# A state update on four groups of array columns, its sum in four pieces, and a new order of the steps

## The chip, the cores and the metric

The kernel runs on one core of a Trainium2 chip. A core has TensorE (matrix products into PSUM; PE in a profile, its weight loads PEld), VectorE (DVE), ScalarE (ACT), GpSimd (POOL) and SyncE (SP), which issues nearly all transfers here. The metric is the device time in microseconds of one launch, lower is better.

## The reference, cut to what matters

Inputs are `q, k, v, a_re, a_im` of shape (4, 8, 768, 48): batch, heads, time, width. A gated linear attention runs over time, and its output feeds a feed-forward block with weights `w_in` (384, 1024), `w_out` (1024, 384) and a gain `g_ln`:

```python
for t in range(S):
    new_re = ar * S_re - ai * S_im          # ar, ai: a at time t, its magnitude kept under 0.999
    new_im = ar * S_im + ai * S_re
    kv = np.einsum('bhd,bhe->bhde', k[:, :, t], v[:, :, t])
    S_re, S_im = (new_re + kv, new_im)
    y[:, :, t] = np.einsum('bhd,bhde->bhe', q[:, :, t], S_re)
...
h = x @ w_in                                # x: y as 3072 tokens by 384
solu = h * softmax(h)
ln = (solu - mean(solu)) / np.sqrt(var(solu) + 1e-06) * g_ln
out = ln @ w_out
```

## The kernel before, in words

**Tiling.** Time is cut into six stretches of 128 steps. A stretch of one batch element is a chunk, so there are 24 chunks, numbered `c` with the batch index running fastest. Two chunks that lie side by side form a group `g` (12 groups), whose gates are worked out together. Every product with 128 output rows is written as products of 32 rows each, so that up to four of them, on four groups of 32 columns of the array, can be under way together.

**Steps of a group** (`prep_steps`, L790 to L990, and `load_steps`): transfers `load_ar`, `load_ai`, `load_q`, `load_k`, `load_v`, `load_vr` (v again, with odd heads in another order); then a chain that goes back and forth between ScalarE and VectorE: `inverse` (ACT, L825), `ratio` (DVE, L831), `sure` (ACT), `tangent` (DVE, L840), `square` and `secant` (ACT), `size` (DVE, L853), `eps` (ACT, L856), `lnm` (DVE, L860), and, from group 3 on, `lh` (ACT, L865) and `ll` (POOL, L870). `total0/1` (PE) sums the logarithms over time, `grow` and `decay` (ACT) take their exponentials, `angle` (ACT, L921), `on` (DVE, L926), `xh` (ACT) and `xl` (DVE, L872) lead to `phase0/1` (PE), `nearest` (ACT), `part` (DVE and ACT), `cos` and `sin` (ACT). `qs` and `ks` (DVE, L909 and L913) scale q and k. `last` and `onward` send the last row of a group on, and `tot` (DVE, L918) turns it into the factor by which the state is scaled.

**Steps of a chunk.** `q2` and `k2` (DVE, L999) make rotated copies with 96 values for each head, `kqb` (DVE, L1008) and the transfer `kqt0` transpose them, `score0/1` (PE, L1053) forms their products in PSUM, `mask0` (DVE, L1058) masks them, and `values` (PE, L1086) forms y in a PSUM tile of the tag `y`, with the state's part. `carry` (PE, L1094) forms the new part of the state, `d = k2^T V`, of 96 rows by 8 heads of 48 columns, in another tile of the same tag; this pool has one buffer, so the two take turns. `add` (DVE, L1103 and L1104) adds it to the state of its batch element and scales the sum; in the first stretch (`ti == 0`) it is one multiplication (L1106). The last stretch has neither, so 20 chunks do.

**Steps of the feed-forward block.** `turned_x` (ACT, L1120) copies y, `up0/1` (PE, L1127), `exp0` (ACT, L1135), `solu` (DVE, L1139), `blocks` (DVE, L1157) and the transfer `away` transpose the result, or `zt0/1` (PE) and `zT0/1` (ACT) in chunks 0, 1, 2 and 23. `centred` and `norm` (POOL), `spread` (ACT, L1173) give the normalization, `down0/1` (PE, L1192) the last product, `scale` (ACT) and `store` the output. In the beginning `fetch`, `raised` and `convert` bring in the weights in seven pieces, `gain` the gain, and `mean`, `meansum`, `centre` prepare `w_out`. `again` and `inspect` read the weights once more for a check of their range; `judge` and `count` gather the checks in a flag.

**What sets the order.** A long string, `ORDER`, lists all 1189 steps; a step is its name and number. The kernel issues them in this order, and every engine and queue works through its own part of it in order. Pieces `fetch:0` and `fetch:3` use the room of a tile that is filled only later (`EARLY`), one after the other; the other pieces share two buffers.

Of the kernel before, what the change touches and what calls it, by code (L numbers as in the profile page):

```python
# [20 lines left out]
P = 128  # L21
# [495 lines left out]
init:0 load_ara:0 load_aia:0 inversea:0 ratioa:0 surea:0 load_arb:0 tangenta:0 inverseb:0 squarea:0 fourtha:0  # L517
load_aib:0 ratiob:0 secanta:0 load_k:0 sureb:0 sizea:0 epsa:0 tangentb:0 fetch:5 squareb:0 lnma:0 secantb:0 sizeb:0
gain:0 total0:0 fetch:1 epsb:0 load_vr:0 lnmb:0 fourthb:0 decay0:0 total1:0 grow0:0 raised:5 decay1:0 grow1:0 trig:0
load_q:0 convert:5 anglea:0 ks1:0 raised:1 angleb:0 fetch:0 last:0 load_ar:1 phase0:0 nearest0:0 convert:1 part0:0  # L520
phase1:0 ks0:0 nearest1:0 qs0:0 sina:0 load_v:0 qs1:0 cosa:0 part1:0 q2:0 raised:0 k2:0 convert:0 load_ai:1 sinb:0
cosb:0 qt0:0 kt0:0 q2:1 exp:0 qT0:0 kT0:0 k2:1 inverse:1 qt1:0 ratio:1 score0:0 kt1:0 qT1:0 kT1:0 fetch:2 score1:0
onward:0 mask0:0 sure:1 tangent:1 kt1:1 values:0 raised:2 fetch:6 qt1:1 square:1 convert:2 kT1:1 turned_x:0 secant:1
raised:6 size:1 carry:1 fetch:3 qT1:1 tot:0 qt0:1 eps:1 convert:6 up0:0 fourth:1 qT0:1 up1:0 lnm:1 raised:3 load_ar:2
convert:3 exp0:0 total1:1 total0:1 grow1:1 decay1:1 load_q:1 decay0:1 load_k:1 grow0:1 trig:1 kt0:1 add:1 solu0:0
angle:1 phase1:1 kT0:1 fetch:4 qs1:1 raised:4 nearest1:1 ks1:1 phase0:1 nearest0:1 carry:0 ks0:1 convert:4 part1:1
part0:1 score1:1 score0:1 mean:0 mean:3 sin:1 add:0 cos:1 load_ai:2 qs0:1 mask0:1 centred:0 mean:1 mean:2 k2:2
load_k:2 mean:6 values:1 exp:1 again:6 again:5 inverse:2 last:1 q2:2 kqb:2 mean:5 mean:7 ratio:2 mean:4 load_v:1
meansum:0 zt0:0 turned_x:1 sure:2 kqt0:2 up0:1 centre:5 centre:2 tangent:2 square:2 zt1:0 zT0:0 up1:1 centre:3
centre:6 score0:2 centre:4 load_vr:1 onward:1 centre:0 load_q:2 secant:2 centre:7 size:2 centre:1 eps:2 score1:2 q2:3  # L530
k2:3 lnm:2 down0:0 load_ai:3 fourth:2 load_ar:3 kqb:3 zT1:0 total1:2 total0:2 exp0:1 decay0:2 solu0:1 decay1:2 grow1:2
kqt0:3 mixed:0 grow0:2 mask0:2 down1:0 trig:2 angle:2 last:2 zt0:1 values:2 on:2 ks0:2 qs1:2 zT0:1 spread:0 phase1:2
phase0:2 tot:1 turned_x:2 up1:2 mixed:1 load_v:2 nearest0:2 nearest1:2 carry:2 part0:2 score1:3 qs0:2 score0:3 part1:2
norm:0 zt1:1 cos:2 add:2 sin:2 exp:2 zT1:1 q2:4 k2:4 inverse:3 centred:1 mask0:3 load_k:3 up0:2 scale:0 values:3
turned_x:3 down0:1 kqb:4 exp0:2 ratio:3 solu0:2 sure:3 kqt0:4 down1:1 tangent:3 ks1:2 square:3 secant:3 size:3
centred:2 spread:1 eps:3 onward:2 carry:3 q2:5 zt0:2 norm:1 lnm:3 add:3 zt1:2 scale:1 load_vr:2 k2:5 lh:3 spread:2
up0:3 up1:3 tot:2 fourth:3 ll:3 score1:4 score0:4 load_q:3 zT0:2 zT1:2 kqb:5 load_ai:4 total1:3 norm:2 total0:3 exp0:3
decay1:3 mask0:4 kqt0:5 decay0:3 grow1:3 solu0:3 grow0:3 down0:2 store:0 inspect:5 trig:3 down1:2 angle:3 values:4
on:3 last:3 xh:3 ks0:3 qs1:3 turned_x:4 xl:3 load_ar:4 blocks:3 phase1:3 scale:2 load_v:3 phase0:3 score0:5 nearest0:3
carry:4 qs0:3 nearest1:3 part0:3 part1:3 sin:3 centred:3 away:3 score1:5 cos:3 up1:4 store:1 add:4 mask0:5 up0:4  # L540
load_k:4 q2:6 k2:6 exp:3 inverse:4 values:5 kqb:6 spread:3 ratio:4 load_q:4 norm:3 exp0:4 turned_x:5 solu0:4 sure:4
tangent:4 kqt0:6 ks1:3 onward:3 square:4 centred:4 secant:4 blocks:4 down0:3 down1:3 size:4 carry:5 q2:7 load_vr:3
eps:4 lnm:4 lh:4 spread:4 up0:5 up1:5 fourth:4 k2:7 ll:4 scale:3 score1:6 score0:6 kqb:7 away:4 load_ai:5 total1:4
norm:4 total0:4 exp0:5 decay1:4 kqt0:7 mask0:6 grow0:4 store:2 down0:4 decay0:4 grow1:4 solu0:5 add:5 blocks:5 down1:4
trig:4 angle:4 values:6 on:4 xh:4 last:4 xl:4 phase1:4 scale:4 ks0:4 load_v:4 qs1:4 turned_x:6 phase0:4 carry:6
score1:7 qs0:4 nearest0:4 nearest1:4 part0:4 part1:4 centred:5 score0:7 tot:3 add:6 sin:4 mask0:7 cos:4 spread:5 up1:6
exp:4 load_ar:5 away:5 store:3 up0:6 load_k:5 q2:8 k2:8 kqb:8 inverse:5 ratio:5 values:7 exp0:6 down0:5 sure:5 kqt0:8
# [64 lines left out]
def whole(ctx, tc, flag, q, k, v, a_re, a_im, moe_w_in, moe_w_out, moe_g_ln, out):  # L612
# [427 lines left out]
    def chunk_steps(c):  # L1040
# [47 lines left out]
        def carry():  # L1088
            V = T["v", g][:, own]
            d = st["d"] = ps_y.tile([D2, DM], FP, tag="y", padded_shape=[P, 512], name="f_d")  # L1090
            for x in range(H):
                hs, k2 = slice(x * D, (x + 1) * D), T["kq", c][:, 0, x]
                for r in range(0, D2, 32):
                    nc.tensor.matmul(out=d[r:r + 32, hs], lhsT=k2[:, r:r + 32], rhs=V[:, hs], start=True, stop=True)  # L1094
# [278 lines left out]
```

## Time and profile before

| | |
|---|---|
| time, median of 3 runs | 415.97 us (414.54 to 417.99) |
| the profiled execution | 416.22 us, span 414.4 us |
| PE busy | 378.1 us (91%) |
| DVE busy | 339.4 us (82%) |
| ACT busy | 296.4 us (72%) |
| POOL busy | 67.6 us (16%) |
| f_d products (`carry`) | 960 records, 18.0 us busy |

The span runs from the first to the last instruction of the profiled execution. A group in the profile is named by line, engine, operation, and the tiles it writes and reads; its busy time is that of one engine, and the idle time beside it is put down to what ended it. A product appears as two records, with one weight load (PEld) each. The chain that ended last goes back from the last instruction to whatever released each step. Busy times of records that overlap on one engine are not to be added up to a span.

### The profile page before, as it was taken

What the parts mean: (1) busy time and instruction counts of PE and PEld (TensorE: products, weight loads), DVE (VectorE), ACT (ScalarE), POOL (GpSimd) and SP (SyncE); (2) the same over time, 40 slices, a digit from 0 to 9 for tenths busy, and PEclk for the clock granted to TensorE, in tenths of its full rate; (3) what the DMA queues carried; (4) which work ended last, traced back from release to release, by engine and by line L of the source; (5) the groups of instructions that cost most, each with busy time, mean ns of one, the idle gap of its engine ahead of it and who ended that gap; (6) DMA issues with size and microseconds to landing.
All of it is one profiled execution on the core that took longest, in us unless ns stands there. A gap on an engine that the chain in (4) does not pass through costs nothing.

```text
span 414.4 us, 15807 instructions
## 1 busy us (share of the span) xinstructions
PE 378.1 (91%) x6908; PEld 202.2 (49%) x6908; DVE 339.4 (82%) x424; ACT 296.4 (72%) x477; POOL 67.6 (16%) x142
## 2 busy tenths in 40 slices
PE   0358689999999999999999999999999999999994
PEld 0026254444645654554554554654644646546553
DVE  3798999697898899898898989998888988865530
ACT  5996967879787778768768878867876867731332
POOL 3000000105032023023023023103023022210111
PEclk9987989999999999999999999999999999999999
DMA  8999849686698788689669679589679579578641
GB/s 218 264 219 264 231 119 199 165 189 140 147 196 181 162 194 180 150 187 204 140 137 210 143 160 225 135 177 205 146 173 232 127 165 200 166 172 236 226 129 49
DMA packets 168703, 74.20 MB, mean 179 GB/s; under 512 B 143537, under 2 KB 156977, under 8 KB 167857
## 3 DMA queue, kind: packets, MB, share of 16 engines
q1 hardware_dynamic: 168336, 72.67, 74.7%
q8 instruction: 56, 0.92, 0.9%
q10 hardware_dynamic: 288, 0.43, 0.3%
q14 instruction: 23, 0.18, 0.1%
HBM read 38.87 MB, written 4.72 MB: 105 GB/s over the span
## 4 chain that ended last, share of the span: by engine, by line
PE 68%; ACT 10%; DVE 9%; DMA 5%; issue 3%; SPq 3%; DVEq 0%; ACTq 0%
PE f_h L1127 23%; PE f_o L1192 22%; PE f_y L1086 8%; PE f_score L1053 6%; PE f_d L1094 3%; PE f_phase L877 2%; PE f_L L877 2%; DMA f_zT<-f_zb 1%; DMA f_kqT<-f_kb 1%; SPq L1162 1%; DMA f_rows<-f_ar 1%; PE f_L L882 1%; DMA f_ar<-in_a_re_dram 1%; PE f_phase L882 1%; SPq L1013 1%
## 5 line engine op out<-in xcount | busy, mean ns | idle before, releaser
L1127 PE MATMUL f_h<-f_w_in,f_xT 128*32 128x512 f32 x1152 | 130.0, 593 | 0.0
L1192 PE MATMUL f_o<-f_w_mix,f_zT 128*32 128x384 f32 x1280 | 108.3, 487 | 0.1
L1127 PEld LDWEIGHTS f_h<-f_w_in,f_xT 128*32 128x32 f32 x1152 | 38.8, 110 | 66.7 <-issue 66.0
L1192 PEld LDWEIGHTS f_o<-f_w_mix,f_zT 128*32 128x32 f32 x1280 | 44.3, 110 | 54.0 <-issue 48.4
L1008 DVE STREAM_TRANSPOSE f_kb<-f_kq 128x1536 f32<-128x1536 f32 x22 | 56.5, 2570 | 3.4 <-issue 2.9
L1170 POOL TENSOR_SCALAR f_less<-f_sum 128x1 f32<-128x1 f32 x24 | 12.3, 514 | 179.4 <-DVE f_z L1139 179.4
L1086 PE MATMUL f_y<-f_att,f_v 128*32 128x128 f32 (+1 forms) x384 | 37.0, 277 | 0.4 <-DMA f_w_mix<-in_moe_w_out_dram 0.3
L1139 DVE SCALAR_TENSOR_TENSOR f_z<-f_h,f_z 128x1024 f32<-128x1024 f32 x24 | 29.2, 1218 | 9.9 <-ACT f_z L1135 9.9
L1053 PEld LDWEIGHTS f_score<-f_kqT 96*32 96x32 f32 x1536 | 32.5, 113 | 9.5 <-issue 8.1
L1086 PE MATMUL f_y<-f_att,f_vr 128*32 128x128 f32 x384 | 37.0, 277 | 0.0
L1135 ACT ACTIVATE f_z<-f_h 128x1024 f32<-128x1024 f32 x24 | 24.3, 1014 | 16.6 <-PE f_h L1127 16.6
L1053 PE MATMUL f_score<-f_kqT 96*32 96x128 f32 (+3 forms) x1536 | 33.9, 239 | 1.4 <-DMA f_kqT<-f_kb 0.8
L1058 DVE TENSOR_TENSOR f_att<-f_score,f_mats 128x1024 f32<-128x1024 f32 x24 | 29.2, 1215 | 7.1 <-PE f_score L1053 6.9
L1086 PE MATMUL f_y<-f_kqT,f_state 96*32 96x128 f32 (+1 forms) x640 | 33.5, 272 | 0.0
L1179 POOL TENSOR_SCALAR f_s<-f_s,f_sum 128x1 f32<-128x1 f32 x24 | 9.9, 413 | 108.3 <-ACT f_z L1173 106.8
L1173 ACT ACTIVATE f_z<-f_z,f_less 128x1024 f32<-128x1024 f32 x24 | 27.3, 1138 | 0.0
L1086 PEld LDWEIGHTS f_y<-f_att,f_v 128*32 128x32 f32 (+1 forms) x384 | 22.6, 105 | 6.3 <-issue 3.9
L1086 PEld LDWEIGHTS f_y<-f_att,f_vr 128*32 128x32 f32 x384 | 22.7, 111 | 5.2 <-issue 5.2
L1157 DVE STREAM_TRANSPOSE f_zb<-f_z 128x1024 f32<-128x1024 f32 x20 | 24.8, 1238 | 0.1
L870 POOL TENSOR_TENSOR f_ll<-f_lr,f_lh 128x768 fp32r<-128x768 f32 x9 | 16.9, 1878 | 46.9 <-ACT f_lh L865 40.2
L1219 ACT ACTIVATE f_ot<-f_o,f_rs 128x384 f32<-128x384 f32 x23 | 13.1, 572 | 14.6 <-PE f_o L1192 7.3
L999 DVE TENSOR_TENSOR f_kq<-f_cs,f_q 128x768 f32<-128x768 f32 x24 | 22.7, 944 | 0.6 <-ACT f_cs L953 0.5
(123 smaller groups left out, 650.3 us busy)
## 6 DMA issues: line engine op xcount, KB each, us to landing
f_kqT<-f_kb SPq DMA_DIRECT2D x88, 192.0 KB, 3.5
f_zT<-f_zb SPq DMA_DIRECT2D x80, 128.0 KB, 3.0
f_raw<-in_moe_w_out_dram SPq DMA_DIRECT2D x14, 384.0 KB, 4.2
f_raw<-in_moe_w_in_dram SPq DMA_DIRECT2D x5, 1024.0 KB, 6.8
f_k<-in_k_dram SPq DMA_DIRECT2D x12, 384.0 KB, 4.9
f_q<-in_q_dram SPq DMA_DIRECT2D x12, 384.0 KB, 5.5
f_v<-in_v_dram SPq DMA_DIRECT2D x12, 384.0 KB, 4.5
out_dram<-f_ot SPq DMA_DIRECT2D x23, 192.0 KB, 3.4
```

The source lines that it names most:

```text
L870: nc.gpsimd.tensor_tensor(out=t, in0=st[src], in1=st[hi].bitcast(FP), op=OP.subtract)
L999: nc.vector.tensor_tensor(out=t, in0=T["cs", g][:, i * H:(i + 1) * H], in1=heads(T[nm, g][:, i]).unsqueeze(2).to_broadcast([P, H, 2, D]), ...
L1008: nc.vector.transpose(out=t, in_=T["kq", c].rearrange("p n h (f j) -> p j (n h) f", j=3))
L1053: nc.tensor.matmul(out=scores[r0:r0 + 32, x, r:], lhsT=QK[:, r // 32, x], rhs=QK[:, r // 32:, H + x], start=True, stop=True)
L1058: nc.vector.tensor_tensor(out=st["att"].rearrange("p (i u) t -> p i u t", u=2), in0=scores.rearrange("p (i u) t -> p i u t", u=2), in1=mat ...
L1086: nc.tensor.matmul(**product)
L1127: nc.tensor.matmul(out=st["h"][r:r + 32, half * 512:(half + 1) * 512], lhsT=st["xT"][:, c * P + r:c * P + r + 32], rhs=w_in[:, c, half * 5 ...
L1135: nc.scalar.activation(out=z, in_=h, func=AF.Exp, accum_out=sums[:, n:n + 1])
L1139: nc.vector.scalar_tensor_tensor(out=st["z"], in0=st["h"], scalar=1.0, in1=st["z"], op0=OP.mult, op1=OP.mult, accum_out=st["sum"][:, 0:1])
L1157: nc.vector.transpose(out=st["zb"], in_=st["z"].rearrange("p (c s f) -> p s c f", s=4, f=32))
L1173: nc.scalar.activation(out=st["z"], in_=st["z"], func=AF.Square, bias=st["less"], accum_out=st["sum"][:, 1:2])
L1192: nc.tensor.matmul(out=st["o"][rows], lhsT=zT, rhs=w[:, c], start=(c == 0), stop=(c == KF - 1))
```

## The change

The update of the state has 24 blocks, three of 32 rows for each of eight heads. Before, the three row blocks of a head stand on three groups of array columns and the heads follow each other in eight rounds. Now heads 0 to 5 stand on the first three groups in six rounds, and the six blocks of heads 6 and 7 stand on the fourth. The PSUM tile is then 128 rows by 288 columns: rows 0 to 95 hold heads 0 to 5, and rows 96 to 127 hold heads 6 and 7, their three row blocks side by side. The sum with the state is made in four pieces: one of 96 rows by 288 columns, and three that read rows 96 to 127 and write the state's rows 0 to 31, 32 to 63 and 64 to 95, 96 columns each. The scaling stays one instruction; in the first stretch there are four multiplications in place of one.

```diff
-            d = st["d"] = ps_y.tile([D2, DM], FP, tag="y", padded_shape=[P, 512], name="f_d")
-            for x in range(H):
-                hs, k2 = slice(x * D, (x + 1) * D), T["kq", c][:, 0, x]
-                for r in range(0, D2, 32):
-                    nc.tensor.matmul(out=d[r:r + 32, hs], lhsT=k2[:, r:r + 32], rhs=V[:, hs], start=True, stop=True)
+            d = st["d"] = ps_y.tile([P, 6 * D], FP, tag="y", padded_shape=[P, 512], name="f_d")
+            queues = [[(x, r) for x in range(6)] for r in range(3)] + [[(6 + x, r) for r in range(3) for x in range(2)]]
+            for n, todo in enumerate(zip(*queues)):
+                for k, (x, r) in enumerate(todo):
+                    nc.tensor.matmul(out=d[k * 32:k * 32 + 32, n * D:(n + 1) * D], lhsT=T["kq", c][:, 0, x, r * 32:r * 32 + 32],
+                                     rhs=V[:, x * D:(x + 1) * D], start=True, stop=True)
...
-            d, tot = pairs(st["d"]), T["tot", g][:, own * H:(own + 1) * H].rearrange("p (i u) -> p i u", u=2)
+            d, tot = st["d"], T["tot", g][:, own * H:(own + 1) * H].rearrange("p (i u) -> p i u", u=2)
...
+            parts = [(slice(0, D2), slice(0, 3), pairs(d[0:D2]))]
+            for r in range(3):
+                parts.append((slice(r * 32, r * 32 + 32), slice(3, 4), pairs(d[D2:P, r * 2 * D:(r + 1) * 2 * D])))
+            for part_, i, x in parts:
+                if ti > 0:
+                    nc.vector.tensor_tensor(out=s[part_, i], in0=x, in1=s[part_, i], op=OP.add)
+                else:
+                    nc.vector.tensor_tensor(out=s[part_, i], in0=x, in1=tot[part_, i], op=OP.mult)
             if ti > 0:
-                nc.vector.tensor_tensor(out=s, in0=d, in1=s, op=OP.add)
                 nc.vector.tensor_tensor(out=s, in0=s, in1=tot, op=OP.mult)
-            else:
-                nc.vector.tensor_tensor(out=s, in0=d, in1=tot, op=OP.mult)
```

The whole of `ORDER` is new as well. These are the stretches that the prediction speaks of, engine by engine. VectorE, from the scores of chunk 14 to those of chunk 16:

```
before  k2:15 lnm:8 tot:7 q2:15 kqb:15 mask0:14 solu0:13 add:13 blocks:13 on:8 qs1:8 xl:8 ks0:8 qs0:8 part0:8 part1:8
        add:14 mask0:15 q2:16 k2:16 kqb:16 ratio:9 solu0:14 tangent:9 ks1:8 blocks:14 size:9
after   lnm:8 q2:15 kqb:15 add:13 mask0:14 solu0:13 qs0:8 on:8 ks0:8 xl:8 ks1:8 blocks:13 part1:8 part0:8
        mask0:15 add:14 qs1:8 tot:8 q2:16 k2:16 ratio:9 kqb:16 tangent:9 solu0:14 size:9 blocks:14 k2:17
```

TensorE, the same part, and the end:

```
before  up0:13 score0:14 score1:14 up1:13 total1:8 total0:8 down0:12 down1:12 values:14 phase0:8 phase1:8 carry:14
        score1:15 score0:15 up1:14 up0:14 values:15 down0:13 down1:13 carry:15
after   up0:13 up1:13 score0:14 score1:14 total1:8 total0:8 down0:12 down1:12 values:14 phase0:8 phase1:8
        score0:15 score1:15 carry:14 up0:14 up1:14 values:15 down0:13 down1:13 carry:15
...
before  down0:21 down1:21 up1:23 up0:23 down0:22 down1:22 zt0:23 zt1:23 count:0 down0:23 down1:23 down2:23
after   up1:23 up0:23 down1:21 zt0:23 down0:22 down1:22 zt1:23 count:0 down0:23 down1:23 down2:23
```

SyncE's queue at the start, and TensorE around the third chunk's update:

```
before  load_k:0 fetch:5 gain:0 fetch:1 load_vr:0 load_q:0 fetch:0 last:0 load_ar:1 load_v:0 load_ai:1 fetch:2 onward:0
        fetch:6 fetch:3 load_ar:2 load_q:1 load_k:1 fetch:4
after   load_k:0 fetch:5 load_q:0 fetch:1 load_vr:0 fetch:0 load_ar:1 load_ai:1 fetch:2 last:0 fetch:3 load_v:0 fetch:4
        onward:0 gain:0 fetch:6 load_vr:1 load_q:1 load_k:1 load_q:2
...
before  zt0:1 values:2 phase1:2 phase0:2 up1:2 carry:2 score1:3 score0:3
after   values:2 zt0:1 carry:2 phase0:2 phase1:2 up1:2 score0:3 score1:3
```

## The prediction

> **What bounds the kernel now.** I read the busy times by stretch first, since a share over the whole span mixes a start, a long regular part and an end. Columns: stretch, its length, then PE, PEld, DVE, ACT and POOL busy in us with instruction counts, the granted clock, DMA share, GB/s.
> ```profile
> 0.00:40.00 40.00, 17.09 (x208) 9.12 (x212) 28.46 (x46) 30.31 (x53) 3.59 (x13) 0.87 0.92 241
> 40.00:110.00 70.00, 63.13 (x1050) 31.05 (x1046) 60.70 (x80) 56.43 (x90) 8.63 (x18) 0.98 0.75 174
> 110.00:350.00 240.00, 238.95 (x4644) 128.63 (x4636) 218.00 (x254) 187.96 (x296) 46.51 (x88) 1.00 0.79 174
> 350.00:402.00 52.00, 52.00 (x894) 28.59 (x884) 31.99 (x44) 18.12 (x32) 7.83 (x20) 1.00 0.68 194
> 402.00:414.40 12.40, 6.96 (x146) 4.85 (x138) 0.29 (x2) 3.58 (x7) 1.04 (x3) 0.93 0.13 41
> ```
> From 110 to 402 us TensorE is idle for 1 us in all, so work taken from it there could count in full. But VectorE is at 218.0 of 240. The waits of VectorE from 105 to 350 us say what its other tenth is (us in total, times, longest):
> ```profile
> DVE f_lr L860 <- ACT f_u L857: 6.2, 8, 1.1
> DVE f_x L926 <- ACT f_x L921: 3.9, 4, 1.6
> DVE f_xl L872 <- ACT f_xh L865: 3.9, 4, 1.0
> DVE f_f L941 <- ACT f_f L937: 3.6, 6, 1.5
> DVE f_lr L853 <- ACT f_u L846: 3.0, 8, 0.7
> ```
> All are round trips to ScalarE, 20.6 us together; none waits for the scores or for the up product. So VectorE is nearly always behind TensorE's data, never short of it: with its round trips it is full too. The chain that ended last agrees. It runs through TensorE but leaves it three times in this part, around 180, 263 and 302 us; the first visit reads (start, length, what):
> ```profile
> 189.36 0.85 DVE f_kq L999
> 190.23 2.73 DVE f_kb L1008
> 192.97 1.11 DVE f_att L1058
> ...
> 197.60 0.95 DVE f_x L926
> 198.63 0.85 ACT f_xh L865
> 199.51 0.97 DVE f_xl L872
> 200.52 0.80 PE f_phase L877 x3
> ```
> So two engines bound the regular part within about 1%, and the change takes from one and gives to the other.
>
> The rows of the parts touched (busy us, mean ns):
> ```profile
> L1094 PE MATMUL f_d<-f_v,f_kq 128*32 128x48 f32 x960 | 18.0, 210 | 0.2 <-ACT f_xT L1120 0.2
> L1103 DVE TENSOR_TENSOR f_state<-f_d,f_state 96x384 f32<-96x384 f32 x16 | 8.8, 549 | 0.0
> L1104 DVE TENSOR_TENSOR f_state<-f_state,f_tot 96x384 f32<-96x384 f32 x16 | 10.1, 628 | 0.5
> L1106 DVE TENSOR_TENSOR f_state<-f_d,f_tot 96x384 f32<-96x384 f32 x4 | 2.2, 550 | 1.2 <-issue 1.2
> ```
> The 960 products are 20 chunks by 24 blocks by two records for each block.
>
> [...]up (48 records of 512 columns) takes 5.15 us and down (64 of 384) 5.16, which is 0.84 ns for each column of a round of four. [...]unheld overlap (a 0.55 us multiplication at 22.78 is followed by the next at 23.25, 0.08 early).
>
> **The state update on TensorE: less.** A block's 48 columns should take 0.84 x 48 = 40 ns in its group. Now 8 rounds by two records = 16 turns: 0.65 us; the chain shows f_d between 0.61 and 0.65 us behind other column-tiled work, and 0.81 behind f_phase, whose products fill the array. In the stamps of the update at 125.2 us three blocks start within 8 ns and the next three 42 ns after the first, so the array's columns set the pace and issue does not: a fourth start fits in. After: 12 turns, 0.51 us at 42 ns. Saved: 4 x 42 = 0.17 us for each of 20 chunks, 3.4 us, of which 16 chunks or 2.7 us lie in the full part. Upper end: 3.4. Lower end: 0, if a fourth stream slows the others; the four-group score products, which keep 0.84 ns for a column (64 records, 1.11 us), speak against it.
>
> **The sum on VectorE: more.** The first piece falls from 384 to 288 elements[...]. Three pieces of 96 elements are new[...]. [...] Their sources start at partition 96 and their targets at 0, 32 and 64[...]. A gain is excluded, as three instructions come in. I take 0.58[...], for want of a row: 9.3 us for the 16 chunks of the full part, 2.3 for the first four, whose one multiplication becomes four.
>
> **New order, VectorE in the regular part: back again.** In the old order one f_kq (0.87 us) lies between `size` (L853) and `lnm` (L860), and ScalarE's two steps between them take 0.94 + 0.94: the 6.2 us row. The new order puts `blocks` (1.16) and an f_kq there, 2.03 us: that wait goes. Between `xl` and `part`, `ks1` and `blocks` (1.63) take the place of two short scalings (0.95): most of the 3.6 us row goes. `solu` (1.2) is now all that lies between `tangent` and `size`, where `ks1` and `blocks` (1.63) were: 0.75 us by 8, 6 us for 3.0. `on`-`xl` keeps one scaling between: 3.9 stays. `on` itself has 8 us of work since `lnm` against some 7 of ScalarE: I leave 1. Sum: 0 + 6 + 3.9 + 0.5 + 1 = 11.4 for 20.6, so 9.2 us back. With 9.3 added, VectorE's full part stays as it is, and TensorE's 2.7 us find no taker: **0**.
>
> **New order, the rest.** The start: `carry:2` moves ahead of both phase products and up1:2; in the old order add:2 stood idle for it from 81.6 to 82.8, so 1.2 us back. `add:0` and `add:1` stand ahead of mask0:1 on a VectorE that is 93 to 99% busy from 40 to 70 us: 1.2 of the 2.3 us lie on the path. The start's loads and conversions are dealt out anew: convert:0 ahead of q2:0, inverse:1 and raised:2 among ScalarE's copies. Worked by hand with the trace's durations I get mask0:0 at 35.6 (was 34.58), up0:0 at 39.2 (was 39.83) and lnm:1 1 us later or less. Half-speed stretches of TensorE lie in it, from 27 to 37 us and for 3.4 us in the fifties; [...] One more or less is worth up to 1.7 us. On SyncE's queue load_q comes before fetch:1, gain goes behind fetch:4, load_ai:1 and fetch:2 go ahead of last:0, and load_v:0 goes behind fetch:3, which must wait for convert:0 to leave their common space (about 27.6): v lands near 33, and values:0 needs it near 37. That cover of 4 us, if gone, costs its excess one to one. Later fetch:6 waits for convert:2's buffer (35.6), and load_vr:1, load_q:1 and load_k:1 behind it for no sooner a use than 47. In the regular part load_q and load_ar go before kqt0, last before load_ai and both stores come together: f_kqT takes 3.5 us to land in either order and nothing waits for it but once (0.8 us). On POOL a norm moves ahead of `ll` (0.25 to 0.57 us by four), inside ScalarE's `fourth`. I count **-1.2** for the start: 1.2 for carry:2, 1.2 for the sums against as much from the freed half-speed stretch and later inspections. On TensorE the scores now go ahead of `carry` in the even chunks from 8 on[...]. The sum must free the PSUM bank before the next `values`: it had 6.3 us for that and has 5.2 (`up` alone), against 1.8 of sum; no cost, and if VectorE is over 3 us late, TensorE stops there. The end: zt0:23 moves ahead of down0:22; the gap of 0.3 us before the last products goes: **-0.3**.
>
> **Sum.** The profiled execution took 416.22 us (span 414.4, 1.8 around it), 0.25 above the median of 415.97. 416.2 + 0 - 1.2 - 0.3 = 414.7 us, in this case's own bounds 412 to 418.
>
> **Rivals.** *TensorE stays the only bound* (0.31). The pieces overlap[...] and TensorE's 2.7 us count in full; with a whole half-speed stretch gone as well (1.7): 414.7 - 2.7 - 0.9 = 411.1. For it: a TensorE at 99.6%[...]. *VectorE becomes the bound* (0.17), the case on the slower side. The place is the state sum:[...] if ScalarE's answers come late enough that only half of the waits go (4.6),[...] 426.5. It decides from where the pieces cost 4.2 us more than the waits give back. For it: no idle time that isn't a round trip; against: the waits that vanish are plain durations. *The milder form* (0.11), all waits returned[...] 418.6. *The update is no faster on four groups* (0.05): as VectorE is the bound in my case, 415 all the same.
>
> **How the numbers follow.** Forecast 0.36, the others as given. About 1% (4.2 us) is what a measurement of this kernel can tell from no change: the three runs lie 3.45 us apart. Below 411.8 lie three quarters of the first rival and a quarter of the forecast: 0.32. Above 420.1 lies the bound of VectorE: 0.17. Between: 0.51. The range leaves out a tenth at each end, inside the two outer cases: 409 to 421.
>
> **What would show it.** f_d at 12 turns, 0.5 us, and its group's busy time hardly less (the same records). Four rows for the sum[...]. The wait of L860 gone, that of L853 doubled, VectorE over 93% busy from 110 to 350. TensorE's idle time there says which rival: near 1 us with a shorter part, the first; 3 us and more, VectorE. I would be wrong through the start, where a transfer or a half-speed stretch can move 2 us that no row fixes.

## The result, and the profile after

The changed kernel takes **420.65 us** (median of six runs, 417.99 to 421.23) where the kernel before takes 415.8 beside it: a ratio of **1.0103, 95% interval 1.0066 to 1.0141**. It is slower by 1.0%, where 414.7 us was forecast. Its profiled execution is the fastest of its six runs, 417.99 us with a span of 416.2, so the profile shows 1.8 us of a difference of 4.9.

The stretches of the changed kernel (columns as before):
```profile
0.00:40.00 40.00, 15.52 (x154) 8.47 (x154) 28.96 (x47) 30.09 (x53) 3.60 (x13) 1.00 0.89 244
40.00:110.00 70.00, 63.61 (x1112) 31.44 (x1112) 63.75 (x93) 57.63 (x92) 7.29 (x17) 1.00 0.76 166
110.00:350.00 240.00, 238.71 (x4600) 133.91 (x4602) 223.38 (x300) 188.14 (x295) 47.43 (x88) 1.00 0.76 171
```
TensorE looks as full as before, 238.71 of 240 us. VectorE rose from 218.00 to 223.38 us, 93% busy. But a nearly full TensorE does not get as much done. Here are the products of `down` alone in the regular part, 16 chunks long (defined below): in the kernel before, in the changed one, and in the changed one with two of the order's moves taken back (`both_moves`, below). Columns: stretch, its length, PE and PEld busy with counts, then clock, DMA share and GB/s.
```profile
98.00:339.50 241.50, 86.63 (x1024) 33.93 (x1024) 1.00 0.78 172
96.90:340.90 244.00, 89.47 (x1024) 38.78 (x1024) 1.00 0.76 172
98.10:344.10 246.00, 85.87 (x1024) 33.64 (x1024) 1.00 0.76 172
```
The same 1024 records are busy for 2.8 us longer in the changed kernel. The cause shows in the stamps: in some chunks one of the four column groups starts behind the others (see the single moves below), and the time until it is done counts as busy.

The rows of the parts touched:
```profile
L1094 PE MATMUL f_d<-f_v,f_kq 128*32 128x48 f32 x960 | 14.3, 207 | 2.3 <-DVE f_state L1110 2.3
L1108 DVE TENSOR_TENSOR f_state<-f_d,f_state 32x96 f32<-32x96 f32 x48 | 12.5, 260 | 0.7
L1112 DVE TENSOR_TENSOR f_state<-f_state,f_tot 96x384 f32<-96x384 f32 x16 | 8.9, 555 | 0.6
L1108 DVE TENSOR_TENSOR f_state<-f_d,f_state 96x288 f32<-96x288 f32 x16 | 7.0, 437 | 0.4 <-PE f_d L1094 0.4
```
The update's busy time fell from 18.0 to 14.3 us: 3.7 for 20 chunks, close to the 0.17 us each that the prediction took. The three small sums cost 260 ns each.

The waits of VectorE from 105 to 350 us (us in total, times, longest):
```profile
DVE f_lr L853 <- ACT f_u L846: 5.4, 8, 0.7
DVE f_f L941 <- ACT f_f L937: 4.1, 6, 1.5
DVE f_xl L872 <- POOL f_s L1186: 2.0, 4, 0.5
DVE f_x L926 <- ACT f_x L921: 1.7, 1, 1.7
DVE f_x L840 <- ACT f_u L835: 1.1, 1, 1.1
DVE f_xl L872 <- ACT f_xh L865: 1.0, 2, 0.5
```
The wait at L860 is gone and the one at L853 has nearly doubled, as forecast. With 0.4 at the sum itself the list comes to 15.7 us (17.7 in a second profiled execution), against 21.1 before and a forecast of 11.4.

The chain that ended last spends more time away from TensorE. The view follows it back only to 197.25 us; from there to 350 us it lies outside TensorE for 87 us in the changed kernel (54 in the second execution, from 199 us on) and for 31 in the kernel before. A single visit is no longer than before (20.6 us from 180 to 200.5 then); there are more of them. The chain is no full account, since it takes one of several nearly equal paths: with the new order alone, which is also slower (below), it is outside TensorE for only 7 us. Its first visit, from 201.54 on (start, length, what):
```profile
201.54 1.02 DVE f_f L941 x2
202.57 0.36 DVE f_state L1108
...
202.95 0.26 DVE f_state L1108
...
203.22 0.26 DVE f_state L1108
...
203.49 0.27 DVE f_state L1108
...
203.79 0.04 DVE f_state L1112
...
214.92 0.06 DVE f_lr L853
...
215.80 0.14 DVE f_zb L1163
...
218.82 0.39 SPq L1168
...
220.54 2.96 DMA f_zT<-f_zb
...
223.55 0.51 PE f_o L1198
```
One sees the sum's four pieces, each starting only when the one ahead is out (in the median chunk 1.30 us from the first to the multiplication). Other steps of VectorE follow, left out here; then come `size`, `blocks` behind it, its transfers, and the product of `down` that waited for the last of them.

**A measure for the regular part.** L860 (`lnm`) runs once a group. From its start in group 3 to its start in group 11, eight groups or 16 chunks, passed 241.5 us before and 244.0 after; a second profiled execution of the changed kernel, taken for this, gave 245.4. Up to group 3 the changed kernel leads by 1.1 us (0.7), and behind group 11 it loses 0.4 (0.6). So the loss lies in the regular part, and this length is given for each run below. It comes from one execution each, and a microsecond is within its scatter: the two of the changed kernel lie 1.4 us apart. The start scatters too: three runs below that have the changed kernel's steps up to group 3 reached it 0.6 us ahead of the kernel before, 0.1 behind and 0.6 behind.

### The profile page after: what moved, and what is told of

It reads as the page before. It is cut to its first block, busy times and chain, and to the rows that moved or that the text cites. A ratio compares the mean times of both kernels' runs of the same rounds, so it can differ in the third digit from the quotient of the medians.

```text
span 416.2 us, 15847 instructions
## 1 busy us (share of the span) xinstructions
PE 378.4 (91%) x6908; PEld 207.0 (50%) x6908; DVE 349.7 (84%) x484; ACT 298.1 (72%) x477; POOL 66.0 (16%) x142
## 4 chain that ended last, share of the span: by engine, by line
PE 30%; DVE 8%; ACT 5%; issue 3%; DMA 2%; SPq 2%; POOL 1%; DVEq 0%; ACTq 0%
PE f_o L1198 13%; PE f_h L1133 7%; PE f_y L1086 4%; DVE f_kb L1008 2%; PE f_score L1053 2%; DVE f_kq L999 1%; POOL f_ll L870 1%; SPq L1168 1%; PE f_phase L877 1%; PE f_L L877 1%; DMA f_zT<-f_zb 1%; DMA f_kqT<-f_kb 1%; ACT f_u L846 1%; DVE f_lr L860 1%; PE f_o L1208 1%
## 5 line engine op out<-in xcount | busy, mean ns | idle before, releaser
L1198 PE MATMUL f_o<-f_w_mix,f_zT 128*32 128x384 f32 x1280 | 111.4, 487 | 0.7 <-ACT f_ot L1225 0.6
L1198 PEld LDWEIGHTS f_o<-f_w_mix,f_zT 128*32 128x32 f32 x1280 | 48.1, 110 | 52.9 <-issue 43.2
L1133 PEld LDWEIGHTS f_h<-f_w_in,f_xT 128*32 128x32 f32 x1152 | 40.6, 110 | 67.7 <-issue 67.0
L1008 DVE STREAM_TRANSPOSE f_kb<-f_kq 128x1536 f32<-128x1536 f32 x22 | 54.4, 2472 | 0.3
L1086 PE MATMUL f_y<-f_att,f_vr 128*32 128x128 f32 x384 | 39.7, 275 | 0.0
L1086 PE MATMUL f_y<-f_kqT,f_state 96*32 96x128 f32 (+1 forms) x640 | 36.6, 272 | 0.0
L1086 PEld LDWEIGHTS f_y<-f_att,f_v 128*32 128x32 f32 (+1 forms) x384 | 23.1, 104 | 6.6 <-issue 5.1
L1086 PEld LDWEIGHTS f_y<-f_att,f_vr 128*32 128x32 f32 x384 | 24.1, 111 | 3.1 <-issue 3.1
L1126 ACT COPY f_xT<-f_y 128x384 f32<-128x384 f32 x24 | 11.4, 474 | 19.8 <-PE f_y L1086 19.7
L1176 POOL TENSOR_SCALAR f_less<-f_sum 128x1 f32<-128x1 f32 x24 | 5.8, 241 | 124.0 <-DVE f_z L1145 124.0
L1086 PEld LDWEIGHTS f_y<-f_kqT,f_state 96*32 96x32 f32 (+1 forms) x640 | 23.3, 106 | 0.1
```

Of the source, the lines that this page charges most:

```text
L1008: nc.vector.transpose(out=t, in_=T["kq", c].rearrange("p n h (f j) -> p j (n h) f", j=3))
L1086: nc.tensor.matmul(**product)
L1126: nc.scalar.copy(out=st["xT"], in_=T["y", n])
L1133: nc.tensor.matmul(out=st["h"][r:r + 32, half * 512:(half + 1) * 512], lhsT=st["xT"][:, c * P + r:c * P + r + 32], rhs=w_in[:, c, half * 5 ...
L1198: nc.tensor.matmul(out=st["o"][rows], lhsT=zT, rhs=w[:, c], start=(c == 0), stop=(c == KF - 1))
```

## The experiments

### The two halves of the change, alone

The code of the changed kernel with the order of before (`update_alone`), the order of the changed kernel with the code of before (`order_alone`), the changed kernel without its three small sums, and the changed kernel itself once more, on one chip.

The third, `new_order_no_small_pieces`, is cut from the changed kernel:
```diff
-            for r in range(3):
-                parts.append((slice(r * 32, r * 32 + 32), slice(3, 4), pairs(d[D2:P, r * 2 * D:(r + 1) * 2 * D])))
```


> The update on four groups and its sum in four pieces, in the order of before. Theory A: some 0.7 us more on VectorE for each of 20 chunks, with none of the round trips saved that the new order saves: 422 to 428 us. Theory B: TensorE's 0.17 us by 20 count and nothing else changes: 412 to 415 us.

> The new order with the update on three groups and its sum in one piece, as before. Theory A (VectorE: the three pieces of 32 rows are held one behind the other, 0.27 us each, and VectorE, already full, passes this on to TensorE): VectorE loses some 0.7 us for each of 20 chunks against the changed kernel, and the waits that the new order saves stay saved, so 413 to 417 us, at or below the kernel before. Theory B (the order is at fault: the start's transfers and conversions, and the queue of SyncE): 419 to 422 us, as slow as the changed kernel or slower, since the update then costs TensorE 3 us more.

> The changed kernel without the three pieces of 32 rows: the state of heads 6 and 7 is not updated, everything else is as in the changed kernel. Theory A: VectorE is free of 0.8 us for each of 20 chunks, TensorE's saving counts: 410 to 414 us. Theory B: 418 to 421 us, the pieces lie beside other work.

> The changed kernel once more, beside the others on the same chip: 420.5 us, 1.0 to 1.2% over the kernel before, and in the profile a start that is later than that of the kernel before, if half-speed stretches of TensorE fall into it (mean clock 0.98).

Measured: update alone **1.0161** [1.0105, 1.0217]; order alone **1.0070** [1.0049, 1.0091]; without the small sums 1.0050 [1.0028, 1.0071] (the state of heads 6 and 7 is left without its new part); the changed kernel again 1.0087 [1.0054, 1.0121].

The update alone (424.57 us) fell in the range of its Theory A; the order alone (420.03) and the changed kernel without small sums (418.91) both fell in that of Theory B, where A had expected a gain. Both halves are slower by themselves, and together they cost less than the two added. The waits of VectorE with the new order alone, in the same stretch as above:
```profile
DVE f_f L941 <- ACT f_f L937: 6.9, 7, 1.7
DVE f_lr L853 <- ACT f_u L846: 6.0, 8, 0.8
DVE f_x L926 <- ACT f_x L921: 5.3, 6, 2.4
DVE f_ai L831 <- ACT f_x L826: 5.1, 8, 0.8
DVE f_xl L872 <- POOL f_s L1180: 2.0, 4, 0.5
DVE f_xl L872 <- ACT f_xh L865: 1.0, 2, 0.5
```
With small ones these are 27.1 us, where the old order had 21.1. L860's 6.2 are gone and L853 rose from 3.0 to 6.0: both as the prediction had worked out. But `ratio` (L831) now waits for ScalarE's `inverse`, a wait that the old order didn't have, since `kqb` stood between; and L941 (`part`) and L926 (`on`) rose where the prediction had them fall. The order gives back nothing by itself.

With the update alone, TensorE's waits from 105 to 350 us show who was behind:
```profile
PE f_L L877 <- POOL f_ll L870: 1.8, 5, 0.5
PE f_score L1053 <- DMA f_kqT<-f_kb: 1.4, 1, 1.4
PE f_phase L877 <- DVE f_xl L872: 1.3, 3, 0.6
```
All three hang on VectorE: `ll` on `lnm`, the transposed inputs on `kqb`, the phase on `xl`. TensorE is 235.17 us busy of 240 there, and the regular part takes 248.1 us.

### What the six rounds are worth without the small sums, in the old order

The order of before, with this taken out of the code of the changed kernel:
```diff
-            for r in range(3):
-                parts.append((slice(r * 32, r * 32 + 32), slice(3, 4), pairs(d[D2:P, r * 2 * D:(r + 1) * 2 * D])))
```


> The new update in six rounds without the three small sums (the state of heads 6 and 7 gets only the product with the total, so this part of the update is left out), in the order of the kernel before. It asks what TensorE's four saved turns per chunk are worth when VectorE carries nothing more than before (its big sum is one quarter smaller). TensorE-bound theory: 0.17 us for each of 20 chunks, up to 3.4 us, come through, 0.991 to 0.995 (412.5 to 414 us beside 416). Theory that no engine alone sets the period and every one is within a microsecond of it: less than a third comes through, 0.997 to 1.001. In the new order the same pair (old update with one sum, new update without small pieces) measured 1.007 and 1.005, so 0.2 per cent came through there.

Measured: 0.9971 [0.9950, 0.9991], regular part 240.1 us. The time falls by 1.2 us, about a third of TensorE's possible 3.4, at the edge of the second theory. The lengths of the regular part can now be set side by side:

```
us, group 3 to group 11     update before   six rounds, no small sums   six rounds, four pieces
order before                    241.5               240.1                      248.1
order after                     245.1               243.4                   244.0, 245.4
```
Down a column: the order costs 3.6 us with the old update and 3.3 without the small sums. Along a row: the six rounds without small sums save 1.4 to 1.7 us for 16 chunks, a tenth of a microsecond each and not 0.17. But they free VectorE too: its large sum is a quarter smaller, and from that sum's start to the multiplication pass 0.48 us in place of 0.58, which is 1.6 us for 16 chunks. So no run here shows whether TensorE's saving brought anything: VectorE's alone is as large as the gain.

The small sums cost 8.0 us in the old order, and 0.6 to 2.0 in the new one. VectorE's waits account for this. With the small sums 1.30 us pass where 0.48 did, 13.1 us for 16 chunks. In the new order its waits fell from 28.8 us without them to 15.7 and 17.7 with them, so all but 0.0 to 2.0 us went into time in which it had stood waiting; in the old order they fell only from 23.1 to 17.5, and 7.5 us are left.

### Why a small sum takes 0.27 us

The changed kernel with its small sums reading and writing the same 32 rows, none needing another's output. Their number and size stay; their rows differ, and so does the tile that they write.

```diff
+    spare = const.tile([32, 3, 1, 2, D], FP, name="f_spare")
...
+                if ti > 0 and r > 0:
+                    nc.vector.tensor_tensor(out=spare[:, r - 1], in0=pairs(d[0:32, (r - 1) * 2 * D:r * 2 * D]),
+                                            in1=s[0:32, 3:4], op=OP.add)
```


> The changed kernel with its three small sums, from chunk 2 on, reading rows 0 to 31 of the update and of the state and writing a spare tile, all on the same 32 rows and none of them needing another's output (the sums of heads 6 and 7 are so left out of the state). It asks why the small sums start 0.26 to 0.27 us apart, which is one's whole length. If one is held until the one ahead is out because of the rows that it reads and writes (partition 96 of the update into rows 0, 32 and 64 of the state), they start 0.17 to 0.20 us apart here and the one before the product with the total keeps its length. If 0.26 us is simply what 96 columns cost in this form, they still start 0.26 us apart. Time within 1 us of the changed kernel (420 to 421) in the second case, 418.5 to 420.5 in the first.

The state sum of one chunk, read from the timeline of VectorE (start, length, what): first in this run, with the three small sums in the second row, then in the changed kernel, with all four sums in the first row:
```profile
237.99 0.46 DVE L1112 TENSOR_TENSOR f_state<-f_d,f_state 96x288 f32<-96x288 f32 x1 [0.17 <-PE f_d L1095]
238.37 0.56 DVE L1109 TENSOR_TENSOR f_spare<-f_d,f_state 32x96 f32<-32x96 f32 x3
238.96 0.56 DVE L1116 TENSOR_TENSOR f_state<-f_state,f_tot 96x384 f32<-96x384 f32 x1
```
```profile
233.46 1.27 DVE L1108 TENSOR_TENSOR f_state<-f_d,f_state 96x288 f32<-96x288 f32 x4 [0.23 <-PE f_d L1094]
234.77 0.55 DVE L1112 TENSOR_TENSOR f_state<-f_state,f_tot 96x384 f32<-96x384 f32 x1
```
By the stamps the small sums start 0.165 us apart here, at 234 ns each, and 0.273 in the changed kernel, at 260: there each starts some 13 ns after the one ahead is out, here before it is out. From the large sum to the multiplication pass 0.95 us, not 1.30. The size and number of the sums are ruled out as the reason. Whether it is the rows or the other target tile was not shown, since the run changes both. With the spare tile a chunk's sum is 0.35 us shorter.

The time did not follow. One run took 421.78 us, regular part 245.9, within the changed kernel's own spread (417.99 to 422.77 over its two sets), where I expected up to 2 us less. So 0.35 us a chunk less on VectorE is worth nothing that one run can show in the new order, while leaving the small sums out altogether gave 0.4 to 0.5%. This fits the table's lower row: VectorE's waits are 23.7 us in this run for 15.7 and 17.7, so the time freed became waiting.

### Single moves of the order, taken back or made alone

Two of the new order's moves lie on the chain shown above: `blocks` of an even chunk stands behind `size`, and SyncE issues `load_vr` right ahead of `away`, which waits on the queue behind it (3.7 us for its four transfers on this visit). The old order has a `load_vr` ahead of `away` too, that of the group before. So putting it behind `away` takes the obstacle off, but makes an order that neither kernel has. VectorE and SyncE around group 7:

```
VectorE
before               k2:12 kqb:12 ratio:7 solu0:10 tangent:7 ks1:6 blocks:10 size:7 k2:13 lnm:7
changed              k2:12 ratio:7 kqb:12 tangent:7 solu0:10 size:7 blocks:10 k2:13 lnm:7
blocks_before_size   k2:12 ratio:7 kqb:12 tangent:7 solu0:10 blocks:10 size:7 k2:13 lnm:7
SyncE
before               kqt0:12 load_vr:6 onward:6 load_q:7 away:10
changed              kqt0:12 load_vr:7 away:10 load_q:8
vr_behind_away       kqt0:12 away:10 load_vr:7 load_q:8
```
`both_moves` has both, `both_moves_old_update` both with the code of before.

> The changed kernel with the transposition of z (blocks) of the even chunks put ahead of size on VectorE again, as in the order before; nothing else is moved. Theory C (in the new order this transposition ends late, its fourth transfer reaches TensorE late, one group of array columns starts the down product 0.35 us behind the others and the state's values wait for it): the transposition ends 1 to 1.7 us earlier, the fourth group starts with the others, and 2 to 4 us are gained: 417 to 419. Theory A (VectorE as a whole sets the pace): the wait of lnm for ScalarE, 6 us in all, comes back and 3 us of the wait of size go: 421 to 424.

> The changed kernel with the four transfers of load_vr put behind the four of away on SyncE's queue, in the six groups where they stood ahead of it; VectorE's order is untouched. Theory C: away is issued as soon as z is transposed, up to 1.6 us sooner, and 2 to 4 us are gained: 417 to 419. Theory A: no change, 420 to 421.5.

> The changed kernel with both moves. Theory C: no late group is left, 416 to 418 us. Theory A: 420 to 424 us.

> The new order with both moves, and the update and sum as before. Theory C: the 3 us that the new order lost with the old update come back, and it is at or below the kernel before: 413 to 416.5. Theory A: as the new order with the old update, 419.5 to 421.

Measured, with the regular part: `blocks` back 1.0100 [1.0066, 1.0134], 245.3 us; `load_vr` back 1.0140 [1.0096, 1.0183], 250.6; both 1.0078 [1.0046, 1.0111], 246.0; both with the old update 1.0043 [1.0022, 1.0065], 242.9. None of the four medians lies in the range of either theory.

In the changed kernel the fourth column group of `down` starts 0.35 us behind the other three in the even chunks, seven times between 132 and 315 us (one of them 0.19); in the kernel before this happens once. The products of a chunk's `down` take 5.37 us from the first start to the last end where all groups start together, and 5.54 to 6.37 in these seven. With both moves taken back it happens never. The busy time of `down` shows what this was worth: 89.47 us in the changed kernel and 89.65 with the order alone, 85.87 and 85.88 with both moves taken back, with the new and the old update. With the old update, 2.2 of these 3.8 us reach the regular part (245.1 to 242.9), more than half of what the order costs there, though by one execution each. With the new update nothing comes of it: TensorE is idle for 5.1 us of the regular part in place of 0.8. With both moves and the new update, rows of the waits of all engines:
```profile
DVE f_lr L861 <- ACT f_u L858: 8.8, 8, 1.1
...
PE f_L L878 <- POOL f_ll L871: 3.5, 6, 1.0
...
PE f_o L1199 <- ACT f_ot L1226: 2.6, 3, 1.3
```
With `blocks` ahead of `size`, `lnm` again waits for ScalarE, 8.8 us, and what hangs on `lnm`, the total `f_L`, is late for TensorE. The late column group was real, but not alone the cause; the next wait took its place.

The move of `blocks` made alone in the kernel before, in seven chunks, one of them shown:
```diff
-tangent:7 ks1:6 blocks:10 size:7 k2:13
+tangent:7 ks1:6 size:7 blocks:10 k2:13
```


> The kernel before with one thing moved: the blocks of the even chunks 4, 8, 10, 12, 14, 16 and 18 stand behind size in the order and not ahead of it; nothing else. Path theory (blocks, then the transfer to the fourth column group, then down): a part of the seven transfers now comes late, TensorE's product f_y or f_o starts up to 0.35 us to 1.2 us later at each, and the kernel is slower, 1.002 to 1.008 (417 to 419.5 us beside 416). Waits theory of the prediction (VectorE's round trip at the size of the group, about 0.7 us in each of nine groups, goes because blocks lies in it no more or is filled by it): faster by 1 to 3 us, or the same, 0.993 to 1.001.

Measured: 1.0053 [1.0025, 1.0080], regular part 242.6. The sign is that of the road, but not by the way I expected: no column group of `down` starts more than 0.11 us behind from 105 to 350 us. The wait has moved instead, and grown:
```profile
DVE f_lr L854 <- ACT f_u L847: 11.1, 8, 1.9
...
DVE f_lr L861 <- ACT f_u L858: 0.2, 1, 0.2
```
`blocks` filled the road from `tangent` to `size` and now fills the one from `size` to `lnm`: 6.2 + 3.0 us of waits became 0.2 + 11.1.

### Moves of `kqb` and `solu0`

A third move taken back (`kqb` ahead of `ratio` again); that with `solu0` ahead of `tangent` as before; and the third move made alone in the kernel before. All have the old update. In these and some other runs the lines stand one later than in the kernel before (`ratio` L832, `tangent` L841, `size` L854, `lnm` L861).

```
three_moves_old_update    k2:12 kqb:12 ratio:7 tangent:7 solu0:10 blocks:10 size:7
solu_between_old_update   k2:12 kqb:12 ratio:7 solu0:10 tangent:7 blocks:10 size:7
old_ratio_first           k2:12 ratio:7 kqb:12 solu0:10 tangent:7 ks1:6 blocks:10 size:7
```


> The new order with the update as it was before (48 full products in eight rounds, one sum), and three of the order's moves taken back: the blocks of an even chunk stand ahead of size again, load_vr behind away, and kqb ahead of ratio in each group. Beside it stands the run with the first two taken back, 1.0043 of the kernel before. Path theory (the order loses because it puts blocks, and with it the transfers and the products of down, and the scaled phase later on a road that TensorE waits for): with the third move gone VectorE no longer stands some 5 us at ratio for the inverse, and the time falls to the kernel before, 0.999 to 1.002 (415.5 to 417 us beside 416). Waits theory (only VectorE's idle sum counts, whichever road it lies on): the third move alone brings about 5 us of 240, in full, to 0.992 (412.5 us). Rest theory (the loss sits in what is still moved: exponentials, norms, stores): no gain from the third, 1.0035 to 1.005.

> The run with three moves taken back and the update as before, with one more: solu0 of the even chunk stands between ratio and tangent on VectorE as in the kernel before, not behind tangent. In the run with three moves VectorE waited 8.8 us in 8 groups at tangent for ScalarE's sure, which reads what tangent overwrites, and with nothing left between the two. If that wait is why the third move made the kernel slower (1.0043 to 1.0202), the time comes back to 1.000 to 1.006 (416.5 to 419 us) and the wait at tangent to under 2 us. If the third move did harm in another way (the scaled inputs of the even chunk came too late, or the fourth column group), it stays at 1.014 to 1.022.

> The kernel before with one thing moved: in groups 2 to 11 kqb of the even chunk stands behind ratio on VectorE and not ahead of it, as in the changed kernel. VectorE then waits at ratio for ScalarE's inverse, some 0.6 us a group by the run of the new order alone (5.1 us in 8 groups). Theory that each cover taken off the road from ratio to down and to the size of the group costs what it covered: 1.003 to 1.010 (417.5 to 420 us). Theory that kqb is better behind ratio (taking it back in the new order made that slower, 1.0043 to 1.0202): 0.995 to 1.001.

Measured: 1.0202 [1.0158, 1.0246], 1.0640 [1.0587, 1.0693] and 1.0620 [1.0549, 1.0691]; regular parts 248.1, 264.8 and 265.2 us. All three times lie outside every expectation. The waits of VectorE say how. Third move taken back:
```profile
DVE f_lr L861 <- ACT f_u L858: 8.8, 8, 1.1
DVE f_x L841 <- ACT f_u L836: 8.8, 8, 1.1
```
`tangent` overwrites what ScalarE's `sure` reads. In the new order `kqb` had covered that: it lay between `ratio` and `tangent`, and the wait passed while it ran. With `kqb` taken away, all eight groups wait 1.1 us. With `solu0` put there as a cover, that wait is gone and another stands in its place:
```profile
DVE f_z L1140 <- ACT f_z L1136: 13.3, 6, 2.5
DVE f_f L942 <- ACT f_f L938: 9.2, 7, 2.2
```
In the new order of ScalarE `exp0`, which `solu0` reads, stands behind `sure` in seven of the nine groups from 3 on. So `solu0` is not ready: VectorE stands in front of it six times, 2.2 us in the mean, and `tangent` and the rest of the group's chain are held behind it. In the kernel before ScalarE makes `exp0` first. And `ratio` ahead of `kqb` in the kernel before:
```profile
DVE f_ai L832 <- ACT f_x L827: 12.7, 7, 2.3
DVE f_f L942 <- ACT f_f L938: 9.6, 7, 2.5
```
The same step without its cover waits some 0.6 us a group at L831 in the new order and 1.8 here, where the other queues stand differently. And it doesn't stay there: all waits of VectorE in the stretch come to 44.5 us, 23.4 more than before, and the regular part is 23.7 us longer. So the same move has no fixed price here; what it costs differs with the rest of the order.

### Is the loss all in the regular part? New start, old rest

The old update; all steps up to `lnm:4` in the new order, all others in the sequence of before.

```
ORDER: the first 381 steps of the changed kernel, then the steps not among them as the kernel before has them
refetch_early: in that, again:5 moved from ahead of inspect:5 to behind again:6
```


> The update as before (eight rounds, one sum). The steps up to the close of the fourth group's size (381 of 1189) stand as in the changed kernel's order, all steps after it in the sequence of the kernel before. Theory that the order's loss lies in the regular part alone: in the run of the new order alone that point came 1.7 us earlier than in the kernel before (96.3 against 98.0 us), and the old regular part then takes its 241.5 us, so the kernel is faster, 0.993 to 0.998 (413.5 to 415.5 us beside 416.3). Rival (the lead is spent by the next wait, because products that the old order did before that point now stand after it, or the other way round): 0.999 to 1.004. If the loss lay in the start and not in the regular part: 1.005 to 1.008.

> The spliced order of the run before it (steps up to the size of group 4 as in the changed kernel, the rest as in the kernel before, update as before) with one step moved: the refetch of weight piece 5 for the final inspection is issued beside that of piece 6, as in the kernel before, and not right ahead of its inspection. In the spliced run VectorE stood 4.0 us at that inspection for the transfer. If that is all that kept the splice from its gain, the regular part keeps the lead of some 1.6 us and the kernel comes to 0.993 to 0.999 (412.5 to 415.5 us beside 415.8), against 1.011. If the lead is lost in the seam anyway, 1.000 to 1.005.

Measured: 1.0110 [1.0056, 1.0164], and with the weights' transfer earlier **0.9985** [0.9964, 1.0005], in the range of its first theory. (The two times that the expectation names belong to the group ahead of the cut; at the cut the run of the order alone led by 0.4 us.) The first lost 4.0 us to one transfer at the seam:
```profile
DVE f_least L767 <- DMA f_raw<-in_moe_w_out_dram: 4.0, 1, 4.0
```
Without that wait the regular part takes 241.5 us, as before, and group 3 is reached 1.9 us sooner. So the start of the new order is no loss, and what the order loses, it loses after the cut, where the regular part lies. 415.08 us is the best of the complete kernels here; the interval does not part it from the kernel before.

### The fourth group's sums off VectorE

```diff
+            late = lates[b]
+            for r in range(3):
+                nc.scalar.copy(out=late[r * 32:r * 32 + 32, 0:2 * D], in_=d[D2:P, r * 2 * D:(r + 1) * 2 * D])
...
+            for n, (part_, i, x) in enumerate(parts):
+                by = nc.gpsimd if n else nc.vector
                 if ti > 0:
-                    nc.vector.tensor_tensor(out=s[part_, i], in0=x, in1=s[part_, i], op=OP.add)
+                    by.tensor_tensor(out=s[part_, i], in0=x, in1=s[part_, i], op=OP.add)
...
+                nc.vector.tensor_tensor(out=s[:, 0:3], in0=s[:, 0:3], in1=tot[:, 0:3], op=OP.mult)
+                nc.gpsimd.tensor_tensor(out=s[:, 3:4], in0=s[:, 3:4], in1=tot[:, 3:4], op=OP.mult)
```


> The new update in six rounds, in the order of the kernel before, with the fourth column group's share taken off VectorE: ScalarE copies its three pieces of 32x96 out to rows 0, 32 and 64 of a tile, GpSimd adds that tile to the state of heads 6 and 7 and multiplies it by the total, VectorE adds and multiplies only heads 0 to 5. VectorE has some 0.25 us less per chunk than in the kernel before and 0.97 less than with the three small sums; ScalarE has three copies of 0.2 to 0.3 us more. Theory that the small sums on VectorE ate TensorE's saving: 0.990 to 0.998 (411.5 to 415 us), as the run without the small sums in the old order (0.9971) or a little better. Rival (ScalarE's copies stand in the road of the groups' round trips, each of which VectorE waits for): 1.003 to 1.020.

Measured: 1.0752 [1.0709, 1.0795], regular part 265.6 us, far outside both theories. The copies themselves are short; the waits are not (first the two groups, then rows of the waits of all engines):
```profile
L1110 ACT COPY f_late<-f_d 32x96 f32<-32x96 f32 x60 | 13.9, 232 | 0.8
L1121 POOL TENSOR_TENSOR f_state<-f_state,f_tot 96x96 f32<-96x96 f32 x16 | 11.6, 723 | 1.3
```
```profile
POOL f_state L1116 <- ACT f_late L1110: 71.9, 14, 10.6
...
DVE f_state L1116 <- ACT f_late L1110: 28.0, 14, 4.5
...
PE f_L L879 <- POOL f_ll L872: 8.3, 6, 1.5
```
VectorE's sum of heads 0 to 5 waits for ScalarE's copies of heads 6 and 7, 2.0 us a time, and GpSimd stands at its sum while `ll` comes behind it. So the run shows that this division is slow, and not what a free VectorE would be worth; that stays with the run without the small sums.

## Why the prediction was wrong

**TensorE's update: right in size, small in effect.** 0.17 us a chunk were saved at the instruction (18.0 to 14.3 us for 20). Without the small sums the regular part fell by 0.09 to 0.11 us a chunk, which is also what the smaller large sum takes off VectorE. So "find no taker" is neither shown nor refuted, and the rival of TensorE as the only bound, with all 2.7 us counted, was too generous. I had said that the group's busy time would hardly fall; it fell by the whole saving.

**The sum on VectorE: mis-sized.** I took 0.58 us a chunk "for want of a row": an estimate of mine that no row of the trace before carries, like the sizes behind the rivals' times. From the large sum to the multiplication now pass 1.30 us where 0.58 did: 0.72 more. Two rows of before allow an estimate: 384 elements take 0.549 us (L1103) and 768 take 0.931 (L831), so 0.10 for each 96, and 0.26 for a sum of 96 where 0.260 was measured. With the pieces one behind the other that makes 3 x 0.26 - 0.10 = 0.68 us. But that they don't overlap no row of before shows; it took the stamps of the changed kernel. For 16 chunks it is 11.5 us by the starts, not 9.3.

**New order, VectorE in the regular part: the step that failed.** It said that 9.2 of 20.6 us of waits come back and cancel the sum. Of its five terms three held or nearly: L860's wait went, L853's went to 6.0 (5.4 with the new update) for 6, and L872's came at 3.0 for 3.9, of which 2.0 are put down to GpSimd. Two did not: L941 measured 6.9 us by itself and 4.1 in the changed kernel for 0.5; L926 5.3 and 1.7 for 1. And a sixth was missing: `ratio` ahead of `kqb` opened a wait for `inverse`, 5.1 us, that the step never looked at, because the waits of before had no row for it. By itself the order raises the waits from 21.1 to 27.1 us and costs 3.6 us in the regular part (ratio 1.0070), where the step had it give. The 15.7 us of the changed kernel come with the small sums, not with the order: without them the same order has 28.8. Beside this, `blocks` and `load_vr` were counted for VectorE's waits alone and not for who waits for them: `away`, and the fourth column group of `down`, late by 0.35 us in the even chunks, with 2.8 us more of busy time for `down`.

**The rest of the sum.** The start was forecast at -1.2 and came at -1.1 and -0.7, with three more executions of the same steps at -0.6, +0.1 and +0.6: the size was met in one of five. With the old update four executions gave -1.6 to -1.9. How much half speed falls into the start doesn't decide it: to 40 us the granted clock was 0.87 before (0.50 from 27.1 to 37.3 us) and in the order alone, which leads by 1.7, and 1.00 in the changed kernel. The end was forecast at -0.3; the whole stretch behind group 11, which holds it, came at +0.4 and +0.6. The regular part was forecast at 0 and came at +2.5 in the profiled execution and +3.9 in its repeat; in the second, -0.7 + 3.9 + 0.6 is its whole difference of 3.8.

**The rivals.** The milder form of VectorE as the bound (418.6) came nearest. Its larger sum on VectorE fits the stamps (0.72 us a chunk more), but it too had all 9.2 us of waits return. The hard form, 426.5, lies near the time of the update alone (424.57), but that is a chance of numbers: it had half of the old waits returned by the new order, and the update alone has the old order.

**What stays open.** Which moves make up the order's 3.6 us; the late column groups look like a part of it (2.2 us with both moves taken back, by one execution each). `blocks` behind `size` costs 0.5% alone in the old order; taking it and `load_vr` back gave 1.0043 for 1.0070 and 1.0078 for 1.0087 to 1.0103, intervals that overlap. Why L941 and L926 wait longer in the new order was not tried, nor what TensorE's six rounds are worth with VectorE's load unchanged.

## What to carry to other kernels

Where two engines are both within a per cent of full, as here, don't book the waits of one as room. Work out for each move which instruction now waits, also where the profile of before shows no wait, since what stood between may have been its cover (5.1 us at `ratio` here). A cover counts only if its own input is ready at that place, which another engine's order decides (13.3 us of waits at `solu0`). Busy time of TensorE can hide a wait of one column group (89.47 us for 86.63 in `down`): compare it for the same products before and after. And the sum split into pieces on different rows cost a full length for each piece here, 0.27 us from start to start, with no overlap.

## What the runs showed of the hardware that I had not expected

- Three small sums of one size start 0.273 us apart where they read rows 96 to 127 and write rows 0, 32 and 64 of the state, and 0.165 where all stand on rows 0 to 31 and write a spare tile; the first follows the large sum by 0.46 and 0.36 us.
- A product on four column groups can start with one group 0.35 us behind, where that group's input lands late, and TensorE shows no idle time for it: its busy time in the stretch is 238.71 us against 238.95, while the same products of `down` take 89.47 us against 86.63.
- One pair of neighbours swapped in VectorE's queue in each of ten groups, with no instruction added, made the kernel 6.2% slower.
